# Feed-forward weights in parts, rows 512 on normalised by GpSimd, VectorE's tiles from the third key chunk on, new planner constants

## The chip, the cores and the metric

The kernel runs on one core of a Trainium2 chip. The core has five engines that work side by side, each in the order of its own instruction list: PE (TensorE, matmuls), ACT (ScalarE, activations), DVE (VectorE), POOL (GpSimd) and SP (SyncE, which here only issues DMAs). Data lie in SBUF (128 partitions); PE writes to PSUM, eight banks of 128x512 float32. The metric is the device time of one execution in microseconds.

## The reference

One layer of two parallel branches on the same normalised rows: attention with 32 query heads and a single key and value head, and a feed-forward part with a squared ReLU.

```python
B, S, D, H = 1, 2048, 640, 32      # Dh = D // H = 20, F = 1536
xn = (x - mean(x)) / sqrt(var(x) + 1e-5)
q = (xn @ wq).reshape(B, S, H, Dh).transpose(0, 2, 1, 3)
k, v = xn @ wk, xn @ wv            # one key and value head for all 32
p = softmax(einsum("bhqd,bkd->bhqk", q, k) * Dh ** -0.5)
o = einsum("bhqk,bkd->bhqd", p, v) # heads side by side again, then @ wo
h = relu(xn @ w1 + b1)
out = x + o @ wo + (h * h) @ w2 + b2
```

All inputs and the output are bfloat16.

## The kernel before, in words

**Tiles.** The 2048 rows are 16 tiles of 128 rows (`st`), four chunks of 512 (`c` for keys, `qc` for queries). A block `b` is one query chunk and a group of four heads: 4 x 8 = 32 blocks. For each block there are 16 key tiles, and for each of these four heads: 64 score tiles of 128 keys x 512 queries. PE computes up to four of them at once in its four row groups (L1131, names `ps<-qT,kT`). The first two blocks are run together, chunk of keys by chunk of keys, so that they can begin when only the first keys are there.

**Two ways to the exponential.** Most score tiles go to ACT, two or three banks in one instruction (L1311, `PT<-ps`). The rest, whole key tiles of four heads, go to DVE: L1408 writes the score as a shifted integer whose bits are a rough exponential (`pbx<-ps`), and three further phases add constants to it (L1429 on DVE, `pbx<-pbx` 128x2048; the last phase mostly in pieces on POOL, L1491). PE multiplies all of them with the values (L1598); the phases use a table `vp` of weighted values, which POOL makes (L834).

**The written order.** A planner in the kernel file builds one list of instructions for each engine. It simulates the engines with fixed costs (`PE512`, `ACT_N`, 600.0 for a 128x512 DVE instruction, landing times of DMAs) and always writes the instruction that could begin first, by priority. `pos()` is the number of blocks passed, with fractions; units such as the feed-forward matmuls, the query projections and the outputs have a position at which they may begin. `PLAN` holds 64 rows of thresholds, one for each half block. On the chip nothing is reordered: an instruction that waits holds up everything behind it on its engine.

**The head.** The rows of x arrive in five DMAs (L591). DVE takes the statistics of a tile (L665, L667), ACT those of tile 2; ACT makes four reciprocal deviations at once (L675, L679). The normalisation L693 may go to DVE or POOL, whichever the planner expects to end first; tile 3 is ACT's (L695). Tiles 0 to 3 are transposed by PE (L752) and copied (L707, L708), tiles 4 to 15 by DMA transposes on SP (`turn`, L713, `xnT<-big`). When the four tiles of a chunk are there, the keys of the chunk are projected (`u_KT`, L763 with `wk_c`, then L787) and the values (`u_V`, L822, L826, then on POOL L830 and L834). Before the first data PE runs 22 warm-up matmuls (L635) and then fillers (L1528, L1527).

**Weights.** `weights()` (L602) waits until all 16 tiles are on their way through the transposes and then issues w1 (L604) and w2 (L605), 1920 KB each, on SP. `wo_load()` (L1058) follows at once with the output weights: one DMA of 600 KB (L1062), eight of 25 KB (L1066) and the bias (L1067). The queries of later blocks are projected into `qpk` (L874) and copied on SP, piece by piece, into `qT` (`spread`, L892). The feed-forward part (`u_FFN`, L911) needs w1, the outputs (`u_OUT`, L988, and its relatives) w2 and the output weights.

Of the kernel before, what the change touches and what calls it, by code (L numbers as in the profile page):

```python
# [14 lines left out]
HPG = 4  # L15
# [27 lines left out]
ACT_N, ACT_0 = 426.6, 63.3  # L43
# [42 lines left out]
PLAN = [dict(zip(PLAN_KEYS, p)) for p in (  # L86
# [70 lines left out]
XRP = 2.0  # L157
PASTEP = .12
# [23 lines left out]
PE512, PE320, PESW, PELAT = 220.0, 140.0, 105.0, 170.0  # L182
# [39 lines left out]
class Sched:  # L222
    ENG = ("pe", "act", "dve", "pool", "sp")

    def __init__(self):
        self.free = {e: 0.0 for e in self.ENG}
        self.lists = {e: [] for e in self.ENG}
        self.order = []
        self.streams = []
        self.mode = None  # L230
        self.rows = None
        self.busy = {e: 0.0 for e in self.ENG}
        self.now = 0.0
        self.win = []
        self.port = 0.0
        self.last_port = None
        self.avail = None
# [17 lines left out]
    def pe_cost(self, r, dur):  # L255
        if r.rows is not None and self.mode == "row" and self.rows is not None and not (set(r.rows) & self.rows):
            return 8.0
        return dur + (PESW if r.mode != self.mode else 0.0)

    def run(self):  # L260
        while self.streams:
# [9 lines left out]
            for st in self.streams:  # L271
# [11 lines left out]
                if rr.under:  # L283
                    below.append((st, max(self.free["pool"], t0, self.port, self.free["dve"])))
                    continue
                best = None
                for k, (eng, dur, lat, ins) in enumerate(rr.alts):
                    est = max(self.free[eng], t0)
                    if eng == "pool" or rr.port:
                        est = max(est, self.port)  # L290
# [37 lines left out]
            op.done = est + max(dur, lat) + (PESW if eng == "pe" and rr.mode != self.mode else 0.0)  # L328
            self.free[eng] = est + dur
            self.busy[eng] += dur  # L330
            if eng == "pool" or rr.port:
                self.port = est + dur
# [16 lines left out]
    def beneath(self, d):  # L349
# [12 lines left out]
        while True:  # L362
            t = max(d.start, self.port, self.free["pool"])
# [21 lines left out]
            self.free["pool"] = self.port = t + dur  # L385
# [89 lines left out]
def bass_parallel_sum__grouped_kv_mqa__dense_activation_squared_relu__prompt_kernel(nc, A_x, A_wq, A_wk, A_wv, A_wo, B_x, B_w1, B_b1, B_w2, B_b2, out):  # L475
    es = ExitStack()
    with es:
# [61 lines left out]
        def have(*names):  # L539
            return all(n in done for n in names)  # L540
# [46 lines left out]
        xland = [4000.0, 4850.0, 8700.0, 12000.0, 15000.0]  # L587

        def x_dma(k):
            a0, a1 = xparts[k]  # L590
            dma("sp", f"x{k}", lambda e: e.dma_start(x_sb[:, a0:a1, :], xv[:, a0:a1, :]), [], xland[k])  # L591
# [3 lines left out]
        dma("sp", "wq", lambda e: e.dma_start(wq_sb[:], A_wq.rearrange("(dt p) n -> p dt n", p=128)), [], 9800.0)  # L595
# [5 lines left out]

        def weights():  # L602
            yield Until(lambda: have(*[f"X{st}" if st < TDMA else f"TE{st}" for st in range(ST)]))
# [1295 lines left out]
```

## Time and profile before

| | |
|---|---|
| time of the runs | 714.97, 716.35 and 718.61 us, median 716.35 us |
| span of the profiled execution | 712.3 us, 23357 instructions |
| granted PE clock, mean over the span | 0.978 |
| busy over the span: PE, DVE, ACT, POOL | 696.2, 665.8, 679.5, 419.8 us |
| first exponential on ACT | 14.49 us |
| keys projected on DVE (L787), chunks 1, 2, 3 | 29.78, 39.05, 52.82 us |
| last DMA transpose issued | 44.07 us |
| w1 and w2 issued | 46.20 and 46.83 us |
| first copy of later queries issued | 55.36 us |

The profile gives every instruction with its engine, line and start. The span reaches from the first to the last instruction; a run's time also holds what lies around it. A busy PE is not a PE at full rate: the granted clock says which part of its pulses it got.

```profile
PE   8897999999999999999999999999999999999998
DVE  6895699999999999999999999999999999989995
ACT  5796699999999999999999999999999999999995
POOL 2373466776766666566766566664776576655600
PEclk9997599999999999999999999999999999999999
DMA  6565211110111111111110112111111011111001
```

Each digit is one fortieth of the span, 17.8 us, in tenths. All that falls below 9 on ACT lies in the first five slices and in the last one.

### The profile page before, as it was taken

What the parts mean: (1) busy time and instruction counts of PE and PEld (TensorE: products, weight loads), DVE (VectorE), ACT (ScalarE), POOL (GpSimd) and SP (SyncE); (2) the same over time, 40 slices, a digit from 0 to 9 for tenths busy, and PEclk for the clock granted to TensorE, in tenths of its full rate; (3) what the DMA queues carried; (4) which work ended last, traced back from release to release, by engine and by line L of the source; (5) the groups of instructions that cost most, each with busy time, mean ns of one, the idle gap of its engine ahead of it and who ended that gap; (6) DMA issues with size and microseconds to landing.
All of it is one profiled execution on the core that took longest, in us unless ns stands there. A gap on an engine that the chain in (4) does not pass through costs nothing.

```text
span 712.3 us, 23357 instructions
## 1 busy us (share of the span) xinstructions
PE 696.2 (98%) x9882; PEld 220.6 (31%) x9882; DVE 665.8 (93%) x1144; ACT 679.5 (95%) x704; POOL 419.8 (59%) x670
## 2 busy tenths in 40 slices
PE   8897999999999999999999999999999999999998
PEld 4231122222222333332222333332223333333334
DVE  6895699999999999999999999999999999989995
ACT  5796699999999999999999999999999999999995
POOL 2373466776766666566766566664776576655600
PEclk9997599999999999999999999999999999999999
DMA  6565211110111111111110112111111011111001
GB/s 197 72 160 166 54 25 25 27 23 12 30 20 23 38 29 39 34 26 39 25 29 17 25 32 48 36 23 42 28 24 24 10 41 27 39 35 50 12 6 40
DMA packets 37954, 29.46 MB, mean 41 GB/s; under 512 B 20218, under 2 KB 33499, under 8 KB 37851
## 3 DMA queue, kind: packets, MB, share of 16 engines
q1 hardware_dynamic: 36539, 27.92, 16.5%
q8 instruction: 79, 1.29, 0.7%
q10 hardware_dynamic: 1312, 0.05, 0.1%
q14 instruction: 24, 0.20, 0.1%
HBM read 10.87 MB, written 2.62 MB: 19 GB/s over the span
## 4 chain that ended last, share of the span: by engine, by line
PE 70%; ACT 16%; DVE 11%; DMA 1%; POOL 1%; issue 1%; SPq 0%; DVEq 0%; POOLq 0%
PE ps L1598 25%; PE ps L1131 22%; PE ps L763 21%; ACT PT L1311 16%; DVE pbx L1408 6%; DVE pbx L1429 3%; PE ps L635 1%; DVE hT_tmp L919 1%; DMA qT<-qpk 1%; POOL big L693 0%; DMA dn<-Tn 0%; DVE qpk L874 0%; DVE Tn L1643 0%; PE ps L1527 0%; SPq L892 0%
## 5 line engine op out<-in xcount | busy, mean ns | idle before, releaser
L1311 ACT ACTIVATE PT<-ps 128x1024 bf16<-128x1024 f32 (+1 forms) x684 | 671.8, 1127 | 17.3 <-PE ps L1131 16.8
L1491 POOL TENSOR_SCALAR pbx<-pbx 128x576 int16<-128x576 uint16 (+15 forms) x487 | 309.8, 655 | 184.4 <-DVE pbx L1429 165.2
L1408 DVE TENSOR_SCALAR pbx<-ps 128x512 int16<-128x512 f32 (+1 forms) x575 | 381.2, 691 | 24.7 <-PE ps L1131 23.2
L1131 PE MATMUL ps<-qT,kT 20*128 20x512 bf16 x2048 | 270.8, 390 | 7.4 <-DMA qT<-qpk 3.7
L1429 DVE TENSOR_SCALAR pbx<-pbx 128x2048 int16<-128x2048 int16 x309 | 210.4, 702 | 0.8
L1598 PE MATMUL ps<-pbx,vp 128*32 128x512 bf16 x1764 | 162.9, 387 | 0.7 <-POOL vp L834 0.5
L1131 PEld LDWEIGHTS ps<-qT,kT 20*128 20x128 bf16 x2048 | 66.9, 91 | 271.5 <-ACT PT L1311 180.0
L1598 PE MATMUL ps<-PT,vx 128*32 128x512 bf16 x1460 | 141.6, 387 | 0.0
L763 PE MATMUL ps<-xnT,w_sb 128*32 128x512 bf16 x960 | 82.9, 399 | 0.6 <-DVE pbx L1408 0.2
L927 POOL TENSOR_TENSOR big<-hT_tmp 128x288 bf16<-128x288 bf16 (+5 forms) x91 | 56.8, 636 | 40.5 <-DVE pbx L1429 36.8
L763 PE MATMUL ps<-w_sb,big 128*32 128x320 bf16 x1536 | 79.7, 302 | 0.0
L1598 PE MATMUL ps<-pbx,vx 128*32 128x512 bf16 x588 | 58.5, 389 | 0.5 <-DVE hT_tmp L919 0.2
L1598 PEld LDWEIGHTS ps<-pbx,vp 128*32 128x32 bf16 x1764 | 43.2, 95 | 48.2 <-issue 33.6
L1598 PEld LDWEIGHTS ps<-PT,vx 128*32 128x32 bf16 x1460 | 37.4, 95 | 43.3 <-issue 33.9
L1659 POOL TENSOR_TENSOR OTs<-Tn,Rb 128x224 bf16<-128x224 f32 (+5 forms) x43 | 32.9, 767 | 16.5 <-DVE pbx L1429 16.5
L763 PEld LDWEIGHTS ps<-w_sb,big 128*32 128x32 bf16 x1536 | 31.2, 95 | 30.8 <-issue 25.4
L919 DVE TENSOR_SCALAR hT_tmp<-ps,b1col 128x512 bf16<-128x512 f32 x48 | 35.5, 739 | 1.7 <-PE ps L763 1.7
L763 PE MATMUL ps<-wo_p,OTp 120*32 120x320 bf16 (+1 forms) x640 | 33.7, 302 | 0.1
L763 PE MATMUL ps<-xnT,wq_sb 128*32 128x512 bf16 (+2 forms) x435 | 32.7, 372 | 0.0
L763 PEld LDWEIGHTS ps<-xnT,w_sb 128*32 128x32 bf16 x960 | 19.5, 95 | 31.7 <-issue 23.5
L1598 PEld LDWEIGHTS ps<-pbx,vx 128*32 128x32 bf16 x588 | 15.2, 95 | 20.5 <-issue 12.7
L1643 DVE COPY Tn<-ps 128x512 f32<-128x512 f32 x29 | 19.7, 680 | 0.7 <-PE ps L1598 0.7
(76 smaller groups left out, 185.3 us busy)
## 6 DMA issues: line engine op xcount, KB each, us to landing
Rb<-Rr SPq DMA_DIRECT2D x29, 256.0 KB
w_sb<-in_B_w_dram SPq DMA_DIRECT2D x2, 1920.0 KB
xres<-in_A_x_dram SPq DMA_DIRECT2D x16, 160.0 KB, 2.6
out_dram<-out_sb SPq DMA_DIRECT2D x16, 160.0 KB
qT<-qpk SPq DMA_DIRECT2D x105, 20.0 KB
pbx<-in_A_x_dram SPq DMA_DIRECT2D x3, 640.0 KB
OTp<-OTs SPq DMA_DIRECT2D x96, 20.0 KB
wq_sb<-in_A_wq_dram SPq DMA_DIRECT2D x1, 800.0 KB
```

The costliest lines, as they stand in the source:

```text
L635: [(lambda e, i=i: e.matmul(ps[:, (2, 4, 5, 6, 7)[i % 5], :], ones_bf[:, :], hT_tmp[:, 0, :], start=True, stop=True)) for i in range(22)]),
L763: return lambda e: e.matmul(ps[32 * j:32 * j + m, b_[0], 0:n], Lj, R, start=first, stop=last, tile_position=(0, 32 * j))
L919: v = yield Req(("dve", 658.0, 742.0, [lambda e: e.tensor_scalar(out=hT_tmp[:, k, :], in0=ps[:, b_[0], :], scalar1=b1col[:, f:f + 1], scal ...
L927: w = yield from pieces(512, 139.0, 1.7, lambda c0, c1: (lambda e: e.tensor_tensor(out=h2T[:, qc % 2, f, c0:c1], in0=hT_tmp[:, k, c0:c1], ...
L1131: ins.append(lambda e, i=i, b=b, t=t, h=h: e.matmul(ps[:, i, :], kT[32 * h:32 * h + DH, t * 128:(t + 1) * 128], qT[32 * h:32 * h + DH, b % ...
L1311: op = yield Req(("act", d_, d_ + 107.0, [lambda e, slot=slot, n=n, src=src: e.activation(out=PT[:, slot:slot + n, :], in_=ps[:, src, :], ...
L1408: return Req(("dve", d_, d_ + 82.0, [lambda e: e.tensor_scalar(out=PB[:, k, hsl, :], in0=ps[:, bk:bk + np_, :], scalar1=OFFS, scalar2=0.0, ...
L1429: return Req(("dve", 600.0, 684.0, [lambda e: e.tensor_scalar(out=PB[:, k, :, :], in0=PB[:, s, :, :], scalar1=PH_D[j], scalar2=None, op0=A ...
L1491: return lambda e: e.tensor_scalar(out=PB[:, k, :, :].rearrange("p h n -> p (h n)")[:, c0:c1], in0=PBU[:, s, :, :].rearrange("p h n -> p ( ...
L1598: ins = [(lambda e, h=h, first=first, last=last: e.matmul(ps[32 * h:32 * h + 32, bk, :], lhs, rhs[h], start=first, stop=last, tile_positio ...
L1643: v = yield Req(("dve", 600.0, 682.0, [lambda e: e.tensor_copy(out=Tn[:, tb, :], in_=ps[:, pvb, :])]), (lambda: None if oldt() is None els ...
L1659: w = yield from pieces(512, 138.0, 2.14, lambda c0, c1: (lambda e: e.tensor_tensor(out=dst[:, c0:c1], in0=Tn[:, tb, c0:c1], in1=Rb[:, a, ...
```

## The change

- **w1** is loaded in five DMAs of 128 rows, the first two behind the transpose of tile 7, the others behind that of tile 11, each once the one before has landed in the plan; **w2** in four parts from position 2.6 on, 0.4 blocks apart; the **output weights** from position 4.4 on, the small ones 0.12 blocks apart. Every reader waits for the part that it reads, or for all.
- **Normalisation** L693 of tiles 4 to 15 always goes to POOL (`XNP`), that of tiles 0 to 2 to DVE.
- **VectorE's score tiles** are not begun before the keys of chunk 2 exist in the plan (`DKEY`).
- **Warm-up**: 16 matmuls over eight banks instead of 22 over five.
- **Planner**: the costs are changed (PE 216 and 136 ns, DVE 598 and 1131, ACT 427.0 n + 49.0, GpSimd's normalisation 691, a start time `T0`, a lag `PORTLAG` between a DVE instruction that holds the port which it shares with POOL and the next POOL instruction, SP's issue times), and 64 rows of thresholds are replaced.

```diff
-ACT_N, ACT_0 = 426.6, 63.3
+ACT_N, ACT_0 = 427.0, 49.0
...
+W1AT = (7, 7, 11, 11, 11)
+NWARM, WARMNS = 16, 6000.0
+W2P, W2AT, W2STEP, WOAT, WOSTEP = 4, 2.6, 0.4, 4.4, 0.12
...
+XNP = tuple(range(4, 16))
+DKEY = 'K2'
+PE512, PE320, PESW, PELAT = 216.0, 136.0, 105.0, 172.0
+PECOL = 10.0
+T0 = 780.0
+PORTLAG = 155.0
+EXPLAT = 120.0
+DV512, DVPAIR, DVLAT = 598.0, 1131.0, 78.0
...
         def weights():
-            yield Until(lambda: have(*[f"X{st}" if st < TDMA else f"TE{st}" for st in range(ST)]))
-            dma("sp", "w1", lambda e: e.dma_start(w1_sb[:], B_w1.rearrange("(dt p) f -> p dt f", p=128)), [done[f"X{ST - 1}"]], 9000.0)
-            dma("sp", "w2", lambda e: e.dma_start(w2_sb[:], B_w2.rearrange("(ft p) d -> p ft d", p=128)), [done[f"X{ST - 1}"]], 16000.0)
+            for k in range(DT):
+                yield Until(lambda: f"TE{W1AT[k]}" in done)
+                dma("sp", W1N[k], lambda e, k=k: e.dma_start(w1_sb[:, k, :], B_w1[128 * k:128 * k + 128, :]), [], 3000.0, 600.0)
+                yield Until(lambda: W1N[k] in done)
+            n = FT // W2P
+            for k in range(W2P):
+                yield Until(lambda: pos() >= W2AT + W2STEP * k)
+                dma("sp", W2N[k], lambda e, k=k: e.dma_start(w2_sb[:, n * k:n * k + n, :], B_w2[128 * n * k:128 * n * k + 128 * n, :].rearrange("(ft p) d -> p ft d", p=128)), [], 5000.0, 600.0)
+                yield Until(lambda: W2N[k] in done)
...
-            alts = [("dve", 400.0, 440.0, [fn]), ("pool", 880.0, 1000.0, [fn])]
-            done[f"X{st}"] = yield Req(alts, (lambda: get(f"R{c}", *([f"N{st}"] if st in ACT_STATS else []))), 10 + st, f"XN{st}", port=True)
+            alts = ("pool", 691.0, 750.0, [fn]) if st in XNP else ("dve", 358.0, 440.0, [fn])
+            done[f"X{st}"] = yield Req(alts, (lambda: get(f"R{c}", *([f"N{st}"] if st in ACT_STATS else []))), 10 + st, f"XN{st}", port=st not in XNP)
...
-                                  512, b_, te4(qc) + [done["w1"]], 4, f"FFN{qc}_{f}")
+                                  512, b_, te4(qc), 4, f"FFN{qc}_{f}", gdeps=[get(n) for n in W1N])
...
-            yield Until(lambda: have("woz", "w2"))
+            yield Until(lambda: have("woz", "w2") and pos() >= WOAT)
...
             for i in range(2 * HPG):
+                yield Until(lambda: pos() >= WOAT + WOSTEP * (i + 1))
...
-                if mine < n * MAXD and (s == cur_a[0] or mine < AHT) and left_sb(s) - HPG * ANS >= (plan("clt") if s < NSB - 1 else CLTL) + backlog():
+                if have(DKEY) and mine < n * MAXD and (s == cur_a[0] or mine < AHT) and left_sb(s) - HPG * ANS >= (plan("clt") if s < NSB - 1 else CLTL) + backlog():
```

More of the change, by code (lines that the diff above doesn't have):

```diff
@@ L225, in __init__ @@
     def __init__(self):
-        self.free = {e: 0.0 for e in self.ENG}
+        self.free = {e: T0 for e in self.ENG}
         self.lists = {e: [] for e in self.ENG}
@@ L257, in pe_cost, with switch @@
             return 8.0
-        return dur + (PESW if r.mode != self.mode else 0.0)
+        return dur + self.switch(r)
+    def switch(self, r):
+        return 0.0 if r.mode == self.mode else PESW + (PECOL if r.mode == "col" and self.mode == "row" else 0.0)
     def run(self):
@@ L283, in run @@
                 if rr.under:
-                    below.append((st, max(self.free["pool"], t0, self.port, self.free["dve"])))
+                    below.append((st, max(self.free["pool"], t0, self.portp, self.free["dve"])))
                     continue
@@ L327, in run @@
             op.start, op.dur = est, dur
-            op.done = est + max(dur, lat) + (PESW if eng == "pe" and rr.mode != self.mode else 0.0)
+            op.done = est + max(dur, lat) + (self.switch(rr) if eng == "pe" else 0.0)
             self.free[eng] = est + dur
@@ L331, in run @@
             if eng == "pool" or rr.port:
-                self.port = est + dur
+                self.port = self.portp = est + dur
+                if eng == "dve":
+                    self.portp += PORTLAG
             if eng == "pe":
@@ L362, in beneath @@
         while True:
-            t = max(d.start, self.port, self.free["pool"])
+            t = max(d.start, self.portp, self.free["pool"])
             best = None
@@ L384, in beneath @@
             op.done = t + max(dur, lat)
-            self.free["pool"] = self.port = t + dur
+            self.free["pool"] = self.port = self.portp = t + dur
             self.busy["pool"] += dur
@@ L600, in bass_parallel_sum__grouped_kv_mqa__dense_activation_squared_relu__prompt_kernel @@
         dma("sp", "b1", lambda e: e.dma_start(b1row[:], B_b1.rearrange("(f p) -> f p", p=128)), (lambda: get("x4")), 2500.0)
+        W1N = tuple(f"w1_{k}" for k in range(DT))
+        W2N = tuple(f"w2_{k}" for k in range(W2P))
         def weights():
-            yield Until(lambda: have(*[f"X{st}" if st < TDMA else f"TE{st}" for st in range(ST)]))
-            dma("sp", "w1", lambda e: e.dma_start(w1_sb[:], B_w1.rearrange("(dt p) f -> p dt f", p=128)), [done[f"X{ST - 1}"]], 9000.0)
-            dma("sp", "w2", lambda e: e.dma_start(w2_sb[:], B_w2.rearrange("(ft p) d -> p ft d", p=128)), [done[f"X{ST - 1}"]], 16000.0)
+            for k in range(DT):
[7 more added lines that the diff above has]
+                yield Until(lambda: W2N[k] in done)
+            done["w1"] = done["w2"] = True
         sc.spawn(weights(), "weights")
@@ L633, in warmup @@
         def warmup():
-            op = yield Req(("pe", 22 * 213.0, 22 * 213.0 + 175.0,
-                            [(lambda e, i=i: e.matmul(ps[:, (2, 4, 5, 6, 7)[i % 5], :], ones_bf[:, :], hT_tmp[:, 0, :], start=True, stop=True)) for i in range(22)]),
+            op = yield Req(("pe", WARMNS, WARMNS + 175.0,
+                            [(lambda e, i=i: e.matmul(ps[:, (2, 4, 5, 6, 7, 0, 1, 3)[i % 8], :], ones_bf[:, :], hT_tmp[:, 0, :], start=True, stop=True)) for i in range(NWARM)]),
                            (lambda: get("warm", "ones")), 0, "warmup", mode="full", cols=11264.0)
@@ L707, in evac_te @@
             d_ = ("dve", 450.0, 490.0, [lambda e: e.tensor_copy(out=dst, in_=src)])
-            a_ = ("act", 600.0, 690.0, [lambda e: e.activation(out=dst, in_=src, func=AF.Identity)])
+            a_ = ("act", 620.0, 710.0, [lambda e: e.activation(out=dst, in_=src, func=AF.Identity)])
             return [d_, a_] if st < 4 else d_
@@ L873, in u_QP @@
                                   512, b_, te4(qc) + [done["wq"]], p, f"QT{qc}_{c0}", nj=nj)
-            v = yield Req(("dve", 600.0, 682.0, [lambda e: e.tensor_scalar(out=qpk[0:32 * nj, k, :], in0=ps[0:32 * nj, b_[0], :], scalar1=QSCALE, scalar2=None, op0=ALU.mult)]),
+            v = yield Req(("dve", DV512, DV512 + 78.0, [lambda e: e.tensor_scalar(out=qpk[0:32 * nj, k, :], in0=ps[0:32 * nj, b_[0], :], scalar1=QSCALE, scalar2=None, op0=ALU.mult)]),
                           [v] + qpres[k].last, EVP, f"QE{qc}_{c0}")
@@ L991, in u_OUT @@
             cs = half(hh)
-            n2 = [[done[f"H{qc}_{f}"]] + ([done["w2"]] if f == 0 else []) for f in range(FT)]
+            n2 = [[done[f"H{qc}_{f}"], done[W2N[f * W2P // FT]]] for f in range(FT)]
             n3 = [get(*tiles_of(qc, t)) + (wo_ops() if t == 0 else []) for t in range(NOT + 1)]
@@ L1002, in u_PA @@
             cs = half(hh)
-            v = yield from groups(g_ffn2(qc, st, cs), 320, b_, [done["w2"]], 4, f"PA_{st}_{hh}", gdeps=[[done[f"H{qc}_{f}"]] for f in range(FT)])
+            v = yield from groups(g_ffn2(qc, st, cs), 320, b_, get(*W2N), 4, f"PA_{st}_{hh}", gdeps=[[done[f"H{qc}_{f}"]] for f in range(FT)])
             v = yield Req(("dve", 398.0, 483.0, [lambda e: e.tensor_tensor(out=part[:, st % 4, cs], in0=ps[:, b_[0], 0:320], in1=xres[:, st % 4, cs], op=ALU.add)]),
@@ L1012, in u_PQ @@
             cs = half(hh)
-            v = yield from groups(g_ffn2(qc, st, cs), 320, b_, [done["w2"]], 4, f"PA_{st}_{hh}", gdeps=[[done[f"H{qc}_{f}"]] for f in range(FT)])
+            v = yield from groups(g_ffn2(qc, st, cs), 320, b_, get(*W2N), 4, f"PA_{st}_{hh}", gdeps=[[done[f"H{qc}_{f}"]] for f in range(FT)])
             done[f"HD{qc}_{st}_{hh}"] = v
@@ L1036, in u_P1 @@
             n3 = [get(*tiles_of(qc, t)) for t in ts]
-            v = yield from groups(g_wo(qc, st, cs, ts) + g_ffn2(qc, st, cs), 320, b_, [done["w2"]] + wo_ops(), 4, f"P1_{st}_{hh}", gdeps=n3 + n2)
-            v = yield Req(("dve", 450.0, 491.0, [lambda e: e.tensor_tensor(out=part[:, st % 4, cs], in0=ps[:, b_[0], 0:320], in1=xres[:, st % 4, cs], op=ALU.add)]), [v, done[f"xr{st}"], olast[(st - 4, hh)]], EVP, f"PE1_{st}_{hh}")
+            v = yield from groups(g_wo(qc, st, cs, ts) + g_ffn2(qc, st, cs), 320, b_, get(*W2N) + wo_ops(), 4, f"P1_{st}_{hh}", gdeps=n3 + n2)
+            v = yield Req(("dve", 398.0, 483.0, [lambda e: e.tensor_tensor(out=part[:, st % 4, cs], in0=ps[:, b_[0], 0:320], in1=xres[:, st % 4, cs], op=ALU.add)]), [v, done[f"xr{st}"], olast[(st - 4, hh)]], EVP, f"PE1_{st}_{hh}")
             done[f"PP{st}_{hh}"] = v
@@ L1254, in poll @@
                     dd = get(*sorted({q for b, tt, h in au for q in qname[b]} | {kn(tt) for b, tt, h in au})) + [o for x in bk for o in bank[x].last]
-                    return Req(("pe", 216.0, 216.0 + PELAT, qk_ins(au, bk)), dd, 0, "QK", mode="row", rows=[h for _, _, h in au], cols=80.0 * len(au), after=t)
+                    return Req(("pe", PE512, PE512 + PELAT, qk_ins(au, bk)), dd, 0, "QK", mode="row", rows=[h for _, _, h in au], cols=80.0 * len(au), after=t)
                 yield Until(lambda: cur_a[0] < NSB or opened or "Dend" in done)
@@ L1405, in ask @@
                 def ask(k=k, hs=hs, bk=bk, b=b, qk=qk, old=old, np_=len(hs)):
-                    d_ = 600.0 if np_ == 1 else 1135.0
+                    d_ = DV512 if np_ == 1 else DVPAIR
                     hsl = slice(hs[0], hs[-1] + 1, hs[-1] - hs[0] if np_ > 1 else 1)
-                    return Req(("dve", d_, d_ + 82.0, [lambda e: e.tensor_scalar(out=PB[:, k, hsl, :], in0=ps[:, bk:bk + np_, :], scalar1=OFFS, scalar2=0.0,
+                    return Req(("dve", d_, d_ + DVLAT, [lambda e: e.tensor_scalar(out=PB[:, k, hsl, :], in0=ps[:, bk:bk + np_, :], scalar1=OFFS, scalar2=0.0,
                                                                               op0=ALU.add, op1=ALU.max)]), [qk] + old, 2 if left_ns(b) > URGN else 0.7, "P1", deadline=lambda: qk.done + SEM_NS + plan("p1tol"))
@@ L1428, in ph_req @@
             k = cur[0]
-            return Req(("dve", 600.0, 684.0, [lambda e: e.tensor_scalar(out=PB[:, k, :, :], in0=PB[:, s, :, :], scalar1=PH_D[j], scalar2=None,
+            return Req(("dve", DV512, DV512 + 84.0, [lambda e: e.tensor_scalar(out=PB[:, k, :, :], in0=PB[:, s, :, :], scalar1=PH_D[j], scalar2=None,
                                                                         op0=ALU.add)]), [acc[-1]] + pbres[k].last, plan("php") if left_ns(b) > URGN else 0.8, "PH", port=True)
@@ L1642, in norm @@
                 return
-            v = yield Req(("dve", 600.0, 682.0, [lambda e: e.tensor_copy(out=Tn[:, tb, :], in_=ps[:, pvb, :])]), (lambda: None if oldt() is None else [pv] + oldt()), 0, f"N1_{b}")
+            v = yield Req(("dve", DV512, DV512 + 78.0, [lambda e: e.tensor_copy(out=Tn[:, tb, :], in_=ps[:, pvb, :])]), (lambda: None if oldt() is None else [pv] + oldt()), 0, f"N1_{b}")
             bank[pvb].last = [v]
@@ L1722, in bass_parallel_sum__grouped_kv_mqa__dense_activation_squared_relu__prompt_kernel @@
                 at = FAT[qc] + f * FSTEP[qc]
-                need = [f"TE{4 * qc + i}" for i in range(4)] + ["w1", "B1"] + [f"TP{i}" for i in range(ST)]
+                need = [f"TE{4 * qc + i}" for i in range(4)] + list(W1N) + ["B1"] + [f"TP{i}" for i in range(ST)]
                 if qc >= 2:
```

20 lines of the change are left out of this document (10 added, 10 removed), and 122 rows, old and new, of the table PLAN.

## The prediction

> **What bounds the kernel now.** I read the busy table in stages first. Its columns are the stretch, its length, then busy time (and count) of PE, weight loads, DVE, ACT and POOL, the granted clock, the DMA share and GB/s.
>
> ```profile
> core 0: us, PE busy (x) PEld busy (x) DVE busy (x) ACT busy (x) POOL busy (x), PEclk, DMA share, GB/s
> 27.40:31.10 3.70, 3.68 (x50) 1.52 (x50) 1.32 (x4) 0.00 (x0) 0.48 (x1) 0.59 0.22 44
> 31.10:53.00 21.90, 20.65 (x276) 6.64 (x274) 20.10 (x37) 20.72 (x24) 15.57 (x22) 1.00 0.61 143
> ...
> 58.30:63.30 5.00, 1.26 (x15) 0.29 (x15) 0.76 (x2) 1.26 (x3) 0.00 (x0) 0.78 0.33 87
> 63.30:90.00 26.70, 26.70 (x209) 5.09 (x205) 18.05 (x29) 18.84 (x18) 10.44 (x16) 0.53 0.27 64
> ...
> 95.00:700.00 605.00, 602.20 (x8703) 188.82 (x8695) 591.62 (x987) 604.76 (x620) 378.25 (x598) 1.00 0.12 28
> ```
>
> From 95 us on ScalarE's exponentials are the bound: ACT is busy 604.76 of 605.00 us, DVE 591.62. What can still be won lies before 95 us: ACT stands still 3.70 us at 27.4 (no keys yet), about 3.7 us at 59, and 26.70 - 18.84 = 7.86 us of the stretch to 90 us, where PE is never idle but is granted 0.53 of its clock. A microsecond won here moves the saturated stretch forward as a whole, so it counts once at the end.
>
> Next the timeline, to see who caused the stop at 59 us.
>
> ```profile
> 46.20 0.59 SPq L604 DMA_DIRECT2D w_sb<-in_B_w_dram  x1
> 46.83 0.52 SPq L605 DMA_DIRECT2D w_sb<-in_B_w_dram  x1
> 47.39 6.14 SPq L1066 DMA_DIRECT2D wo_p<-in_A_wo_dram  x4
> 53.57 1.45 SPq L1066 DMA_DIRECT2D wo<-in_A_wo_dram  x4
> ...
> 55.36 10.47 SPq L892 DMA_DIRECT2D qT<-qpk  x14
> ...
> 62.58 0.61 PE L1131 MATMUL ps<-qT,kT 20*128 20x512 bf16 x3 [3.74 <-DMA qT<-qpk]
> ...
> 63.24 2.11 ACT L1311 ACTIVATE PT<-ps 128x1024 bf16<-128x1024 f32 x2 [3.74 <-PE ps L1131]
> ```
>
> Both weight matrices (L604, L605) and the small output-weight loads (L1066) stand in SP's queue ahead of the query copies of the next block (L892). The first copy goes out at 55.36 and the DMA engines are full (1.06 share, 369 GB/s at 53 to 58.3 us). PE waits 3.74 us, and afterwards the same three score matmuls take 0.61 us instead of 0.39.
>
> Last, the line that the change moves between engines, all its instances; durations are minimum, median and maximum in ns.
>
> ```profile
> L693 DVE TENSOR_SCALAR big<-pbx,mv,rstd x12: 430/440/580, 7.4 to 41.2; 128x640 bf16<-128x640 bf16 x12
> L693 POOL TENSOR_SCALAR big<-pbx,mv,rstd x2: 2506/2584/2663, 16.9 to 40.8; 128x640 bf16<-128x640 bf16 x2
> L713 SPq DMA_TRANSPOSE xnT<-big x12: 1200/1276/2399, 19.6 to 44.1; - x12
> L1491 POOL TENSOR_SCALAR pbx<-pbx 128x640 int16<-128x640 uint16 x5 | 3.6, 723 | 4.8 <-DVE pbx L1408 2.8 <-DVE pbx L1429 2.1
> ```
>
> VectorE normalises a tile in 0.44 us, GpSimd in 2.51 and 2.66 us. GpSimd does as many elements (128x640) of another scalar instruction (L1491) in 0.72 us. The planner of the changed kernel counts 0.691 us.
>
> **The change part by part** (minus is a gain; against the profiled span of 712.3 us).
>
> 1. *Weights no longer ahead of the query copies.* w1 goes out as five parts behind the transposes of tiles 7 and 11, w2 as four parts from position 2.6, the output weights from 4.4 on, one by one. The stop at 59 us loses its cause: **-3.7** (ends: 0 if another transfer is late there, -4.2, the idle time that DVE shows before the same matmuls). What stays on SP: five w1 issues of about 0.55 us (L604: 0.59, L605: 0.52), 2.8 us between transposes of 1.28 us each, and 1.92 MB, which at the 350 to 370 GB/s of 50 to 58 us need 5.3 us of all DMA engines. Nothing waits for them while the transposes wait for GpSimd anyway (item 4): 0. Without that cover at most three parts, 3.2 us, come ahead of the last transposes. A w2 part (480 KB, 1.4 us) can hold a query copy for 1.4 us; each block has some 20 us, so 0.
>
> 2. *The half clock after that stop.* It began with the 4.2 us in which PE did nothing, so it goes with it: **-7.9** of ACT time (ends: 0 if a new stop takes its place, -8.65 = 26.70 - 18.05 on DVE).
>
> The Trainium skill, "TensorE: Matmul & The Clock Gate", Part 1, has the clock halved after an idle window of about 3.4 us and restored after as much sustained work. The trace agrees with the drop and not with the return: 0.53 over 26.7 us of busy PE. By that rule this item would be some 1 us instead of 7.9, as an estimate from that page.
>
> 3. *Head.* 16 warm-up matmuls instead of 22: the last ones run at 0.22 us, so PE is free 1.3 us earlier; the first transposes start at 9.79 us, right behind warm-up (L635) and filler (L1528). The chain then needs query weights that may land at the same time as before: **-0.5** (0 to -1.3).
>
> 4. *GpSimd normalises tiles 4 to 15.* In both measured cases VectorE's L693 ran beside it, 1.14 us in the first (17.82 to 18.96 us) and 0.44 us of work in the second. That is gone now. Taking these off leaves 1.5 and 2.07 us; I take **2.07** (nearest to its own row), ends 0.72 (L1491) and 2.66. Four tiles, then, feed one chunk of 512 keys every 8.3 us, where the transposes need only 4 x 1.28 = 5.1 us. Per chunk 3.2 us late, for three chunks 9.5 us. PE executes in the written order; the key projections K1 to K3 stand where 0.691 us would put them, and everything behind them waits, the score matmuls and so ACT too. Of this 3.7 us are already paid today (ACT idle 27.40 to 31.10, for K1): **+5.8** (ends: at 0.72 us no lateness and that wait goes too, -3.7; at 2.66 us 3 x 4 x 1.38 - 3.7 = +12.9). Queued behind these on GpSimd are the value tables L834 (0.41 us each), which the tile products of VectorE's share need.
>
> The Trainium skill, "GPSIMD Engine Reference", Engine selection, calls one-input work on GpSimd roughly line rate, and its side-by-side accounting gives 1.03 cycles per element for short bodies, by estimate 0.55 us for 640. L1491 agrees, L693 does not. By that rule item 4 is the lower end.
>
> 5. *VectorE's tiles begin after K2.* Today L1408 and L1429 take 3.8 us from 20 to 31 and 6.1 us from 31 to 41: 9.9 us that start later. Ten normalisations leave DVE: 10 x 0.44 = 4.4 us. The other 5.5 us must be fitted in later, where DVE has 605 - 591.6 = 13.4 us idle: **+1** (0 if all fits; +2.8 if ACT and DVE share the whole of it).
>
> 6. *New cost constants and 64 rows of thresholds.* They change order and shares, no instruction's time. ACT waits 0.2 us in all from 95 to 700 us, so order can win nothing there; only exponentials moved to DVE's 13.4 idle us could: 0 (ends -5 and +5: a tile costs DVE 4 x 0.68 for L1408 and, with 309 L1429 to 147 tiles, 2.1 x 0.70, so 4.2 us, and spares ACT four exponentials of 671.8/1460 = 0.46 us; 13.4 us hold three tiles, 5.5 us of ACT; a worse order costs as much).
>
> Sum: -3.7 - 7.9 - 0.5 + 5.8 + 1 = **-5.3 us**, span 707.0. The runs' median is 716.35, 4.05 above the profiled span; I leave that difference, so **711.0 us**, 0.7% faster.
>
> **The rivals.**
>
> *GpSimd at the cheap price.* For: L1491, and L693 was only seen beside VectorE's own. Against: in the second case one L693 of 0.44 us can't explain 1.8 us. Then -3.7 - 7.9 - 0.5 - 3.7 + 1 = -14.8: **701.5 us**.
>
> *Slower: PE in order behind the key projections.* At 2.51 us and more per tile each chunk is 4 x 1.23 = 4.9 us late, as long as the 4.2 us stop that cost PE its clock. Then item 4 is 3 x 4.9 - 3.7 = +11.0, and the last stop, in front of K3, leaves a half clock like today's, so item 2 is 0: -3.7 + 0 - 0.5 + 11.0 + 1 = +7.8: **724 us**. It decides from about 2.3 us per tile on, where a chunk's lateness passes 4 us. For: both measured instances are above. Against: fillers (L1527) stand dense there, and the clock came back at once after the K1 wait (0.59 to 31.1, 1.00 after).
>
> *The change doesn't win what it says.* The wait on the query copies moves to other copies, or the thresholds cost what the weights give: items 1 and 2 halve to -5.8, the rest is +6.3: **717 us**. For: the copies still queue behind five w1 parts. Against: w2 and the output weights, two thirds of the bytes, are far away.
>
> **How the numbers follow.** The forecast 0.43 (its own range 705 to 716), cheap price 0.20, slower 0.24, no gain 0.13. A change within 0.5% (712.8 to 719.9) can't be told from none. Faster by more: 0.43 x 0.8 + 0.20 + 0.13 x 0.2 = 0.57. Slower: 0.24 x 0.9 + 0.13 x 0.3 = 0.26. The rest, 0.17, is within. The range 699 to 723 takes in the cheap price and most of the slower case.
>
> **What would show it.** L693 on POOL x12 with its duration: 2.07 is my step, under 1 or over 2.4 the rivals. The starts of the three L787 (today 29.8 and 39.05 and 52.82) say how late the chunks are; ACT's idle time ahead of each should sum to about 9.5 us. No wait on qT near 59 us and clock 1.00 from K3 to 95 us show items 1 and 2. I am wrong if the clock falls again after a key projection, if ACT is under 99.5% from 95 us on, or if the chunks come as early as the transposes allow.

## The result, and the profile after

The changed kernel takes 748.52 us (median of four runs, 744.91 to 750.26), the kernel before 717.0 beside it: 1.0451 of the time, 95% interval 1.0395 to 1.0506. The profiled span went from 712.3 to 743.2 us, +30.9. A kernel's runs can fall into two groups some 2% apart; ratios compare the lower ones, and where a profile is of the upper group its span is named.

First the busy table of the changed kernel in stages; the columns are those of the table in the prediction.

```profile
core 0: us, PE busy (x) PEld busy (x) DVE busy (x) ACT busy (x) POOL busy (x), PEclk, DMA share, GB/s
24.00:31.50 7.50, 2.84 (x38) 1.00 (x42) 0.24 (x1) 2.51 (x4) 7.29 (x7) 0.50 0.45 99
31.50:55.50 24.00, 21.18 (x177) 4.66 (x175) 6.64 (x11) 15.35 (x15) 21.50 (x19) 0.50 0.55 122
55.50:100.00 44.50, 44.50 (x317) 7.59 (x315) 21.65 (x31) 29.35 (x29) 13.81 (x22) 0.50 0.08 22
100.00:112.00 12.00, 11.96 (x113) 2.44 (x109) 8.68 (x16) 9.09 (x10) 3.69 (x6) 0.66 0.14 25
...
120.00:700.00 580.00, 573.81 (x8043) 173.58 (x8039) 558.17 (x925) 579.87 (x601) 341.95 (x570) 1.00 0.14 32
```

TensorE runs at 0.50 of its clock from 22.8 us, just ahead of this table, to 108.1 us. From 55.5 to 100 us it is busy for all 44.50 us and ScalarE for 29.35: the exponentials wait for score matmuls, and neither keys nor queries nor a DMA is missing. From 24 to 55 us GpSimd is the engine that is busy nearly throughout, 28.79 of 31.50 us. From 120 us on the picture is that of before: ACT 579.87 of 580.

Next the instances of the moved line, and of the transposes behind it (durations minimum/median/maximum in ns, then first and last start).

```profile
L719 POOL TENSOR_SCALAR big<-pbx,mv,rstd x12: 2498/2500/2509, 17.1 to 46.1; 128x640 bf16<-128x640 bf16 x12
...
L739 SPq DMA_TRANSPOSE xnT<-big x12: 1199/1201/2267, 19.7 to 48.7; - x12
```

A normalisation on GpSimd takes 2.50 us, whether VectorE is busy beside it (all of 17 to 19 us) or hardly at all (0.24 of the 7.50 us from 24 us on). Twelve of them end at 48.6 us, and each transpose follows its tile. The keys are projected on DVE at 34.05, 44.18 and 55.52 us (before: 29.78, 39.05, 52.82).

Third the timeline of PE and ACT around the first of these waits (start, duration, instruction; in brackets the idle time before it and what ended it).

```profile
22.65 1.34 PE L1554 MATMUL ps<-kT,zeros 128*32 128x512 bf16 x12
23.92 0.61 PE L1158 MATMUL ps<-qT,kT 20*128 20x512 bf16 x4
...
24.57 1.94 ACT L1338 ACTIVATE PT<-ps 128x1024 bf16<-128x1024 f32 x2
29.74 0.70 PE L848 MATMUL ps<-wv_c,xnT 128*128 128x20 bf16 x20 [4.66 <-DMA xnT<-big]
...
31.57 1.02 ACT L1338 ACTIVATE PT<-ps 128x1024 bf16<-128x1024 f32 x1 [5.06 <-PE ps L1158]
...
33.07 1.02 ACT L1338 ACTIVATE PT<-ps 128x1024 bf16<-128x1024 f32 x1 [0.48 <-PE ps L1158]
...
34.58 1.02 ACT L1338 ACTIVATE PT<-ps 128x1024 bf16<-128x1024 f32 x1 [0.48 <-PE ps L1158]
```

Four score matmuls take 0.61 us at 23.92, where at full clock (13.41 us) they took 0.39: the clock had fallen already, at 22.8 us. Then PE waits 4.66 us for a transposed tile and ACT 5.06 us behind it. After that ACT gets one exponential per 1.5 us.

Last the two groups of ACT and PE that say how much work ScalarE has, and the end of the chain of waits (start, length, engine and line, instructions).

```profile
L1338 ACT ACTIVATE PT<-ps 128x1024 bf16<-128x1024 f32 (+1 forms) x698 | 683.4, 1224 | 32.4 <-PE ps L1158 31.9
...
L1625 PE MATMUL ps<-PT,vx 128*32 128x512 bf16 x1484 | 149.8, 399 | 2.3 <-ACT PT L1338 2.3
```

```profile
729.84 9.42 PE ps L789 x263
739.43 0.72 DVEq L493
740.15 0.80 DVE out_sb L1000 x2
```

PE multiplies 1484 score tiles that ACT made, 1460 before: 24 tiles, or six key tiles of four heads, went from VectorE to ScalarE. And behind the last exponential (its end is at 729.39 us) 263 output matmuls are left in the chain, where before it was 156 in 5.34 us. So the 30.9 us come from three places on ScalarE, here with the version of run 9 beside it:

| us | before | after | GpSimd in the fast form |
|---|---|---|---|
| idle ahead of the exponentials | 17.3 | 32.4 | 1.5 |
| ACT busy in all | 679.5 | 689.5 | 684.7 |
| from the last exponential to the end | 9.0 | 13.8 | 13.8 |
| span | 712.3 | 743.2 | 708.1 |

+15.1, +10.0 and +4.8 make 29.9 of the 30.9.

### The profile page after: what moved, and what is told of

The parts are those of the page before. It is cut to its first block, busy times and chain, and to the rows that moved or that the text cites. A ratio compares the mean times of both kernels' runs of the same rounds, so it can differ in the third digit from the quotient of the medians.

```text
span 743.2 us, 23093 instructions
## 1 busy us (share of the span) xinstructions
PE 721.1 (97%) x9796; PEld 218.2 (29%) x9796; DVE 648.2 (87%) x1107; ACT 689.5 (93%) x715; POOL 404.8 (54%) x654
## 4 chain that ended last, share of the span: by engine, by line
ACT 78%; PE 16%; POOL 3%; DMA 2%; issue 0%; DVE 0%; SPq 0%; DVEq 0%
ACT PT L1338 78%; PE ps L789 6%; PE ps L1158 5%; PE ps L1625 5%; POOL big L719 3%; DMA wq_sb<-in_A_wq_dram 1%; DMA xnT<-big 0%; PE ps L1554 0%; SPq L607 0%; PE ps L848 0%; POOL vp L860 0%; DVE out_sb L1000 0%; DVEq L493 0%; DVE pbx L1435 0%; ACT rstd L705 0%
## 5 line engine op out<-in xcount | busy, mean ns | idle before, releaser
L1338 ACT ACTIVATE PT<-ps 128x1024 bf16<-128x1024 f32 (+1 forms) x698 | 683.4, 1224 | 32.4 <-PE ps L1158 31.9
L1435 DVE TENSOR_SCALAR pbx<-ps 128x512 int16<-128x512 f32 x544 | 368.7, 702 | 46.2 <-PE ps L1158 42.4
L1518 POOL TENSOR_SCALAR pbx<-pbx 128x384 int16<-128x384 uint16 (+10 forms) x463 | 272.1, 607 | 226.8 <-DVE pbx L1456 222.1
L1158 PE MATMUL ps<-qT,kT 20*128 20x512 bf16 x2048 | 283.3, 398 | 4.4 <-ACT PT L1338 2.0
L1456 DVE TENSOR_SCALAR pbx<-pbx 128x2048 int16<-128x2048 int16 x310 | 203.3, 682 | 0.8
L1625 PE MATMUL ps<-pbx,vp 128*32 128x512 bf16 x1692 | 159.3, 391 | 0.4 <-DVE pbx L1456 0.4
L1625 PE MATMUL ps<-PT,vx 128*32 128x512 bf16 x1484 | 149.8, 399 | 2.3 <-ACT PT L1338 2.3
L953 POOL TENSOR_TENSOR big<-hT_tmp 128x256 bf16<-128x256 bf16 (+5 forms) x93 | 57.2, 627 | 45.3 <-DVE pbx L1456 40.8
L789 PE MATMUL ps<-w_sb,big 128*32 128x320 bf16 x1536 | 79.6, 302 | 0.0
L789 PEld LDWEIGHTS ps<-w_sb,big 128*32 128x32 bf16 x1536 | 32.9, 95 | 28.2 <-issue 21.1
L1686 POOL TENSOR_TENSOR OTs<-Tn,Rb 128x320 bf16<-128x320 f32 (+4 forms) x41 | 32.2, 795 | 9.8 <-DVE pbx L1456 9.8
L719 POOL TENSOR_SCALAR big<-pbx,mv,rstd 128x640 bf16<-128x640 bf16 x12 | 29.9, 2501 | 2.1 <-ACT rstd L705 2.1
```

The lines of the kernel that those rows point to most:

```text
L719: fn = lambda e: e.tensor_scalar(out=xn_sb[:, st, :], in0=x_sb[:, st, :], scalar1=mean, scalar2=rstd[:, st:st + 1], op0=ALU.subtract, op1= ...
L789: return lambda e: e.matmul(ps[32 * j:32 * j + m, b_[0], 0:n], Lj, R, start=first, stop=last, tile_position=(0, 32 * j))
L953: w = yield from pieces(512, 139.0, 1.7, lambda c0, c1: (lambda e: e.tensor_tensor(out=h2T[:, qc % 2, f, c0:c1], in0=hT_tmp[:, k, c0:c1], ...
L1158: ins.append(lambda e, i=i, b=b, t=t, h=h: e.matmul(ps[:, i, :], kT[32 * h:32 * h + DH, t * 128:(t + 1) * 128], qT[32 * h:32 * h + DH, b % ...
L1338: op = yield Req(("act", d_, d_ + EXPLAT, [lambda e, slot=slot, n=n, src=src: e.activation(out=PT[:, slot:slot + n, :], in_=ps[:, src, :], ...
L1435: return Req(("dve", d_, d_ + DVLAT, [lambda e: e.tensor_scalar(out=PB[:, k, hsl, :], in0=ps[:, bk:bk + np_, :], scalar1=OFFS, scalar2=0.0 ...
```

## The experiments

The first theory was the prediction's slower rival made larger: GpSimd at 2.5 us a tile starves PE, PE loses its clock, and a PE at half clock can't feed ScalarE. The rivals were VectorE's late tiles, and the new costs and thresholds. Ratios are to the kernel before, run beside each (714.7 to 715.4 us).

**1. VectorE normalises again**, all else changed.

```diff
-XNP = tuple(range(4, 16))
+XNP = ()
```

> The changed kernel, but VectorE normalises tiles 4 to 15 too (XNP empty). Theory 1, GpSimd's 2.50 us per tile delays the keys and costs PE its clock: the three key copies (L813) come before 45 us, no wait of PE over 3 us on a key transpose, half clock under 15 us, time 700 to 712 us. Theory 2, the late begin of VectorE's tiles thins PE's work and so loses the clock: half clock for over 40 us still, time 730 us or more.

729.51 us, 1.0198 (1.0160 to 1.0237). GpSimd's share is over half of the loss, but some 15 us stay. In the profile (span 743.4) the clock is 0.50 from 28.7 to 66.1 us, though the keys come at 29.3 to 47.7 us; on the mean it is 0.961 there and 0.984 to 0.988 in the other three runs, which so had less half clock.

**2. VectorE's tiles from the start**, GpSimd normalising.

```diff
-                if have(DKEY) and mine < n * MAXD and ...
+                if mine < n * MAXD and ...
```

> The changed kernel without the condition on the keys of chunk 2: VectorE's tiles may begin as early as before; GpSimd still normalises. Theory 1: GpSimd's 12 x 2.50 us stay, keys as late as in the changed kernel (L813 last at 50 us or later), half clock for over 40 us, time 735 to 750 us. Theory 2: clock back by 60 us, time under 722 us.

737.71 us, 1.0323 (1.0287 to 1.0358), half clock from 26.6 to 74.3 us. The later start costs some 10 us while the keys are late.

**3. The kernel before, only the normalisation of tiles 4 to 15 moved to GpSimd.**

```diff
-            alts = [("dve", 400.0, 440.0, [fn]), ("pool", 880.0, 1000.0, [fn])]
+            alts = ("pool", 691.0, 750.0, [fn]) if st >= 4 else [("dve", 400.0, 440.0, [fn]), ("pool", 880.0, 1000.0, [fn])]
```

> The kernel before with one part of the change, tiles 4 to 15 normalised by GpSimd, priced 691 ns in the plan. Theory 1: keys of the last chunk at 50 us or later, PE loses its clock before 45 us for over 40 us, time 730 to 750 us. Theory 2: the tiles of VectorE begin early here, so the clock holds and only some 6 us are lost, time 718 to 726 us.

741.66 us, 1.039 (1.035 to 1.043). Its stages:

```profile
24.00:32.00 8.00, 3.95 (x29) 0.94 (x29) 2.39 (x10) 2.15 (x4) 7.79 (x6) 0.62 0.25 51
32.00:55.00 23.00, 18.87 (x166) 4.16 (x162) 10.76 (x18) 13.11 (x15) 22.68 (x19) 0.50 0.31 57
...
65.00:80.00 15.00, 15.00 (x109) 2.62 (x106) 6.05 (x9) 10.12 (x10) 2.09 (x2) 0.50 0.31 75
```

This one line brings nearly all of the loss, with the thresholds, weights and start of tiles of before: a GpSimd busy from 24 to 55 us and a PE at 0.50. The new planned price moves other work too (ScalarE gets 16 score tiles more), so run 9, which leaves that price alone, is the cleaner proof.

**4. The kernel before, only the weights in parts.**

```diff
+W1AT = (7, 7, 11, 11, 11)
+W2P, W2AT, W2STEP, WOAT, WOSTEP = 4, 2.6, 0.4, 4.4, 0.12
...
-            dma("sp", "w1", lambda e: e.dma_start(w1_sb[:], ...
+            for k in range(DT):
+                yield Until(lambda: f"TE{W1AT[k]}" in done)
+                dma("sp", W1N[k], lambda e, k=k: e.dma_start(w1_sb[:, k, :], ...
```

> The kernel before with the weights part alone: w1 in five, w2 in four parts, the output weights late, all else as before. Step 1 and 2 of the prediction: the 3.74 us wait on the query copies near 59 us and the half clock from 63 to 90 us go, 11.6 us less: 703 to 708 us. Rival, the wait moves to other copies or the clock falls anyway: 714 to 720 us.

709.92 us (10 runs), 0.9933 (0.9901 to 0.9966).

```profile
55.00:65.00 10.00, 9.51 (x115) 2.54 (x112) 8.60 (x14) 10.00 (x12) 5.35 (x9) 1.00 0.09 22
65.00:80.00 15.00, 11.89 (x147) 3.19 (x144) 11.70 (x21) 11.58 (x12) 7.30 (x11) 0.95 0.26 64
80.00:100.00 20.00, 20.00 (x248) 5.11 (x245) 18.64 (x31) 18.95 (x21) 14.02 (x22) 0.95 0.27 72
```

```profile
77.58 0.25 DVE L1661 RECIPROCAL rd<-dn 128x16 f32<-128x16 f32 x1 [3.27 <-DMA dn<-Tn]
...
78.43 1.47 PE L775 MATMUL ps<-xnT,w_sb 128*32 128x512 bf16 x12 [3.11 <-DVE pbx L1421]
```

From 55 to 65 us ACT is busy for all 10 us, where before it was 6.19; the clock is 0.95 from 65 to 100 where before it was 0.50 and 0.79. In this profile items 1 and 2 of the prediction hold in the main when nothing else is changed: ACT gains 7.6 of the forecast 11.6 us from 24 to 100 us. Near 77 us a new wait stands in the way: VectorE waits 3.27 us for the copy of the softmax denominators (`dn`), PE 3.11 us behind it, and the clock is 0.50 again from 78.5 to 81.8 us.

The median is 4.8 us better, between the two expectations. The profiled run (705.22 us, span 703.4) is one of the quickest. The clock reads 0.50 or 1.00 outside the moment of a switch, so the time at half clock is about 2 x (1 - mean clock) x span; for the changed kernel this gives 86 us, and the profile shows 85. For run 4 it gives 7 us in the profiled run but some 20 us in the median one (0.986), against some 31 before (0.978).

**5. Both: VectorE normalises, and its tiles begin at the start.**

> The changed kernel with both taken back, VectorE normalises and its tiles may begin early; weights in parts, 16 warm-up matmuls, new costs and thresholds stay. If GpSimd's price and the late begin are the whole loss: the time of the weights part alone, 705 to 712 us, clock held from 32 us on. Rival, the new costs and thresholds lose the rest: 718 to 728 us, with DVE under 96% from 200 to 600 us.

720.29 us (8 runs), 1.0076 (1.0043 to 1.0109). The clock is 0.54 from 24 to 32 us and 1.00 after that. So without lateness and with half clock only from 21.1 to 31.4 us the changed kernel still loses to the weights alone; what is left of the change in it are costs, thresholds and warm-up. VectorE is busy for 181.9 of the 200 us from 200 to 400, where before it was 195.6.

**6. GpSimd's normalisation priced at what it takes**, so that the order fits it.

```diff
-            alts = ("pool", 691.0, 750.0, [fn]) if st in XNP else ("dve", 358.0, 440.0, [fn])
+            alts = ("pool", 2450.0, 2510.0, [fn]) if st in XNP else ("dve", 358.0, 440.0, [fn])
```

> The changed kernel with GpSimd's normalisation priced at 2450 ns in the plan instead of 691; the instructions on GpSimd stay. If the loss comes from the written order (PE held in front of key projections that stand too early): no wait of PE over 2 us on a transpose, clock held past 30 us or back by 60 us, 715 to 730 us. If the late keys cost it whatever the order: still 50 us and more at half clock, 738 to 752 us.

790.09 us (763.86 to 797.01); the runs lie too far apart for a ratio, but the quickest is still slower than the changed kernel. Neither expected time came. In the profile (span 795.3) PE waits 0.7 us at most for a transposed tile, so the true price does put the late work in its right place; but ACT waits 72.5 us on score matmuls and the clock falls again and again, to 0.92 on the mean from 120 to 700 us. The 64 rows of thresholds were laid against the other price. Why it is so much worse isn't settled.

**7. The changed kernel and 16 dense matmuls (128 rows, 128 columns, 512 wide) behind the third chunk of keys**, whose results nobody reads.

```diff
+        U(-3 + 0.1 * 3 + 0.07, "BURST", ["K3", "V3", "TE0", "TE1", "TE2", "TE3", "ones"], lambda b_: u_BURST(b_))
```

> The changed kernel with 16 dense 128x128x512 matmuls more, behind the keys and values of the last chunk, their result thrown away. If the half clock lasts because the work of PE after the waits is too thin to lift it, the burst lifts it near 60 us instead of 107 us: 12 to 18 us less than the changed kernel, 730 to 738 us. If the clock returns by its own time or the half clock is not what costs, 745 us or more.

736.61 us, 1.0307 (1.0258 to 1.0355): some 12 us come back by work that is added. The first fence has the burst's instances, the second the stages around it.

```profile
L933 PE MATMUL ps<-xnT,ones_bf x16: 379/379/634, 65.7 to 69.7; 128*128 128x512 bf16 x16
```

```profile
65.70:67.00 1.30, 1.30 (x8) 0.47 (x5) 0.00 (x0) 0.57 (x1) 0.00 (x0) 0.50 0.07 16
67.00:70.00 3.00, 3.00 (x14) 1.18 (x12) 0.00 (x0) 0.00 (x0) 0.00 (x0) 0.95 0.12 27
70.00:74.00 4.00, 3.97 (x55) 1.05 (x54) 2.73 (x5) 3.55 (x4) 1.24 (x2) 1.00 0.03 7
```

The clock is back 1.6 us into the burst, at 67.3 us instead of 108.1, and stays. The keys are as late as in the changed kernel (34.0 to 55.5 us), so from there on it was no longer lateness that held the clock down: denser work ended it.

**8. What the 2.50 us are made of.** Seven GpSimd instructions in the head of the kernel before, written to memory that is filled later; one run, 730.1 us.

> The kernel before with seven GpSimd instructions more near 8 us, results unused: the normalisation of 640 columns (scalars from SBUF), the same of 320, with two immediate scalars (subtract and multiply, add and multiply), with one, the int16 form of L1491, a copy. If the scalars read from SBUF make it slow: 2.50, 1.3, then 0.7 to 0.8 us for the rest. If bfloat16 does: all but the int16 form and perhaps the copy at 2 us and more.

```profile
7.68 2.51 POOL L612 TENSOR_SCALAR w_sb<-pbx,mv,rstd 128x640 bf16<-128x640 bf16 x1 [3.69 <-ACT rstd L694]
10.18 1.44 POOL L613 TENSOR_SCALAR w_sb<-pbx,mv,rstd 128x320 bf16<-128x320 bf16 x1
11.59 2.35 POOL L614 TENSOR_SCALAR w_sb<-pbx 128x640 bf16<-128x640 bf16 x1
13.91 0.73 POOL L615 TENSOR_SCALAR w_sb<-pbx 128x640 bf16<-128x640 bf16 x1
14.60 1.82 POOL L616 TENSOR_SCALAR w_sb<-pbx 128x640 bf16<-128x640 bf16 x1
16.39 0.73 POOL L617 TENSOR_SCALAR w_sb<-pbx 128x640 int16<-128x640 uint16 x1
17.06 0.80 POOL L618 COPY w_sb<-pbx 128x640 bf16<-128x640 bf16 x1
```

In order: subtract and multiply with scalars from memory (2.51), the same on half the columns (1.44), subtract and multiply with constants (2.35), **add and multiply with constants (0.73)**, multiply alone (1.82), add and multiply on integers (0.73), a copy (0.80). It isn't the type that makes the price, and the scalars' place is only 0.16 us of it: it is the operations.

**9. The changed kernel with GpSimd in the form add, multiply.** One small VectorE instruction per chunk makes the negated means.

```diff
+            done[f"M{c}"] = yield Req(("dve", 70.0, 150.0, [lambda e: e.tensor_scalar(out=nmr[:, a0:a1], in0=mv[:, a0:a1, 0], scalar1=-1.0, scalar2=None, op0=ALU.mult)]), ...
...
+            fn_p = lambda e: e.tensor_scalar(out=xn_sb[:, st, :], in0=x_sb[:, st, :], scalar1=nmr[:, st:st + 1], scalar2=rstd[:, st:st + 1], op0=ALU.add, op1=ALU.mult)
...
-            alts = ("pool", 691.0, 750.0, [fn]) if st in XNP else ("dve", 358.0, 440.0, [fn])
+            alts = ("pool", 691.0, 750.0, [fn_p]) if st in XNP else ("dve", 358.0, 440.0, [fn])
...
```

> The changed kernel, but GpSimd normalises in the form that took 0.73 us in the probe: x + (-mean), times 1/std, with the negated means made by one small VectorE instruction per chunk. Its price is then the 0.69 us that the plan believed. Theory 1 (GpSimd's 2.5 us price starves TensorE from 24 us on and is the root of the long half clock): normalising takes 0.73 us each, the keys come near where VectorE would have brought them, half clock no longer than in the run with VectorE normalising (65 us), time 715 to 730. Rival (GpSimd's place in the queue, not its price, is at fault; or the late tiles of VectorE and the thresholds are): 735 or more, and half clock past 80 us.

709.79 us, 0.9906 (0.9860 to 0.9951), with every other part of the change in place: the lowest ratio of all, though its interval overlaps run 4's. It went past its own expectation. Four of the five runs took 709.0 to 709.8 us; the fifth took 734.91 at a mean clock of 0.956, so a long half clock is still possible here, while all four runs of the changed kernel have one (0.931 to 0.943). The moved line's instances, then the stages.

```profile
L728 POOL TENSOR_SCALAR big<-pbx,nmr,rstd x12: 873/873/875, 17.7 to 29.0; 128x640 bf16<-128x640 bf16 x12
```

```profile
24.00:31.50 7.50, 7.01 (x92) 2.31 (x84) 1.54 (x3) 7.04 (x11) 7.07 (x11) 0.93 0.94 191
31.50:55.50 24.00, 22.91 (x306) 6.73 (x308) 15.62 (x26) 23.63 (x26) 7.49 (x17) 1.00 0.44 94
55.50:100.00 44.50, 43.12 (x549) 12.01 (x547) 41.91 (x70) 44.50 (x47) 28.24 (x45) 1.00 0.27 68
```

0.87 us instead of 2.50, the last tile at 29.0 instead of 46.1, keys at 28.8 to 41.8, the clock at 0.93 and 1.00, ACT 44.50 of 44.50. One operation name in one instruction, with its negated means, decides 38.7 us (748.5 to 709.8). Even here the clock falls, at 21.6 us, and the timeline of PE shows it return at 25.0:

```profile
23.61 0.62 PE L1634 MATMUL ps<-PT,vx 128*32 128x512 bf16 x4
24.01 1.30 PE L1563 MATMUL ps<-kT,zeros 128*32 128x512 bf16 x12
25.25 0.40 PE L1167 MATMUL ps<-qT,kT 20*128 20x512 bf16 x4
```

Behind twelve fillers the next matmuls take 0.40 us instead of 0.62. PE had worked without a break since 21.23 us. In the changed kernel the same twelve fillers ran at 22.65, and 2.3 us after its clock fell PE stood waiting for a tile.

**10. Run 5 with the 64 rows of thresholds of before** (the table is swapped, the costs stay).

> The changed kernel with VectorE normalising, VectorE's tiles from the start, and additionally the table of thresholds of before; what is left of the change are the weights in parts, the new planned costs, the warm-up and the first exponentials. If the thresholds lose the 10 us between that run (720.3) and the weights alone (709.9): 707 to 713. If the costs and the warm-up lose them: 718 to 724. If costs and thresholds only fit each other: over 724.

756.3 us (744.15 to 764.58), 1.0422 (1.0356 to 1.0488). The thresholds alone aren't what run 5 loses: with the new costs the old ones are, by the two ratios, some 25 us worse than the new. ACT waits 26.9 us on score matmuls in its profile, and the clock dips again at 80 to 100 us (0.83) and around 430. This is the third expectation, that costs and thresholds only fit each other.

**11. The weights alone (run 4), and GpSimd may take chunks 1 to 3 in the fast form, priced 0.70 us beside VectorE at 0.40.**

> The kernel before with the weights in parts, where GpSimd may also normalise chunks 1 to 3 in the add-multiply form at a planned 0.70 us, beside VectorE at 0.40 us, whichever the plan finds sooner free. If the keys wait for normalised rows before 63 us: earlier keys, half clock in 24 to 32 us shorter, 700 to 707. If VectorE alone already keeps pace with the x transfers: 708 to 713, the time of the weights alone.

721.93 us (713.37 to 740.6, 12 runs), 1.0041 (0.9999 to 1.0084). Neither expectation held. The mean clock goes from 1.00 in the quickest runs to 0.957 in the slowest. The three runs at 0.999 and above, the profiled one among them, take 713.4 to 714.1 us, so even at full clock the order that comes of the choice is worse than run 4's.

**12. Run 9 with VectorE's tiles from the start.**

> The changed kernel with GpSimd in the add-multiply form (709.8 us in the run before this one), and VectorE's tiles from the start. If the later start of VectorE's tiles costs time by itself, since ScalarE then has some 6 more key tiles to do: 700 to 706. If the thresholds were fitted to the later start, as the run with VectorE normalising and early tiles suggests (720.3): 713 to 724. If the start makes no difference once the keys come on time: 707 to 712.

732.44 us (12 runs), 1.0033 (0.9991 to 1.0075). Four runs took 715 to 723 us at a mean clock of 0.985 to 0.990, eight 731 to 742 at 0.949 to 0.967; the profile (span 730.4) has the clock at 0.50 from 35.3 to 79.6 us. The four lie in the second expectation, thresholds fitted to the later start. So beside run 9 the later start costs nothing; but of runs 1 and 5, which normalise on VectorE, the one with the early start is 9 us quicker (729.5 and 720.3). What the start is worth by itself stays open.

## Why the prediction was wrong

It said 711.0 us and 0.7% faster; it came 4.5% slower. **The step that failed is item 4's price**, "Taking these off leaves 1.5 and 2.07 us; I take 2.07". The two measured instances, 2.51 and 2.66 us, were full prices: against the 2.50 of the changed kernel, VectorE's own instruction beside them can have cost 0.01 and 0.16 us, not the 0.44 and 1.14 that were taken off. The row taken as the lower end, L1491 at 0.72, was another pair of operations (run 8). With 2.50 the item is 3 x 4 x 1.23 - 3.7 = +11.0, the slower rival's own term, and that rival's bound, 2.3 us, was passed. It had the path right, PE in written order behind the key projections and a half clock, and was wrong in size, 724 for 748.5.

**Item 2 failed with it.** "It goes with it: -7.9" holds in run 9's profile and in part in run 4; in the changed kernel the clock fell 38 us earlier, at 22.8 us, and stayed down for 85 us where before it was 27. It fell 2.3 us ahead of the first long wait for a tile (25.08 to 29.74 us), behind idle gaps of at most 0.95 us in which PE waited for ACT: lateness didn't start this half clock, it came in where run 9's clock returned. The prediction's argument against this, that the clock had come back at once after the wait for the first chunk, was a case of dense work: the trace has 44 matmuls in the 3.3 us from 27.1 to 30.4 us before, and 317 in the 44.50 us of the changed kernel.

Of the 36.2 us between the forecast span and the measured one, items 1, 2 and 4 are 20.9: together they were forecast at -5.8, and the idle time ahead of the exponentials grew by 15.1. The rival, with the right price and no gain in item 2, comes to +7.3 there; that the longer half clock is the rest fits, but isn't measured by itself.

By the Trainium skill, "TensorE: Matmul & The Clock Gate", Part 1, sustained work of about 3.4 us should bring the clock back. The half clocks of 27.1 to 30.4 us before, 27.3 to 30.6 and 78.5 to 81.8 us in run 4 and 21.6 to 25.0 us in run 9 agree, each 3.3 to 3.4 us long with PE busy nearly throughout; the 44.50 us of unbroken busy time at 0.50 after 55.5 us don't. There the trace has 7.1 matmuls per us, in those stretches 7.9 to 14.8; thin work may be the reason, but what the gate counts isn't shown by any run here. The drop doesn't keep to an idle window of that length either: before, the clock fell at 61.1 us, 2.3 us into the stop.

The Trainium skill, "GPSIMD Engine Reference", Engine selection, has one-input work at roughly line rate. Run 8 agrees for add and multiply (0.73 us) and the copy (0.80), and not for the normalisation's subtract and multiply (2.35 to 2.51).

**Item 1** (-3.7) was right in its cause: run 4 and the changed kernel have no wait on the query copies near 59 us, though run 4 has the new wait near 77. **Item 3** (-0.5) held: the first exponential of the changed kernel is at 13.84 us, before at 14.49; in run 9 it is at 14.40. **Items 5 and 6** (+1 and 0) were too small: ACT's 10.0 us more work and the 4.8 us behind the last exponential are theirs. Item 5 isn't needed for ScalarE's six key tiles more: runs 5 and 12, whose tiles start early, give it nine and seven more than before. Run 11, with the costs, thresholds and start of before, gives it seven more as well, so a changed order is enough; which part does it in the changed kernel stays open. In run 9, where nothing is late, ACT is idle 15.8 us less, as items 1 and 2 and the 3.7 us of the first chunk's wait together had said (15.3); but ACT is 5.2 us busier, with the six more key tiles among its work, and 4.8 us more lie behind the last exponential. So the cheap rival's 701.5 is 709.8. That 709.8 stands close to the forecast of 711.0 is chance: two errors cancel.

## What to carry to other kernels

Before an operation is moved to another engine, read its own instances there at full price, contention or not, and doubt a cheaper row with other operations; then try its algebraic neighbours, x + (-m) for x - m, before giving up. A wait of some microseconds ahead of TensorE is to be priced with the half clock that it can start or prolong, for that can cost more than the wait; whether a long half clock comes can differ from run to run (runs 4, 9 and 12), so the clock of every run is read, not only that of the profile. A planner's table of thresholds belongs to its costs and its schedule: one changed price (run 6), one table swapped (run 10) or one choice added (run 11) cost more here than the best edit won.

## What was not expected of the hardware

GpSimd's two-operation instruction has a fast pair and slow ones at one shape and type: add and multiply 0.73 us, subtract and multiply 2.35, and multiply alone, with less to do, 1.82. With scalars from memory and VectorE at work beside it the fast pair took 0.87. And TensorE can stay at half its clock for over 40 us without an idle microsecond in the profile (55.5 to 100 us of the changed kernel); in run 7, 16 dense matmuls ended such a stretch within 1.6 us. The clock can also fall without a long stop: at 22.8 us it fell behind gaps of at most 0.95 us.
